# Attention and expert routing on one core: row transposes spread between layer products, second-layer weights moved up

## The chip, the cores and the metric

The kernel runs on one core of one Trainium2 chip. Five engines work side by side and are joined by semaphores only: TensorE (PE in the profile, PEld for its weight loads), VectorE (DVE), ScalarE (ACT), GpSimd (POOL) and SyncE (SP). The metric is device time in microseconds (us) from start to end of one execution; less is better.

## The reference, cut to what matters

```python
# q, k, v: (4, 8, 768, 64) float32; is_retrieval: 8 heads; n_sink = 4, window = 64
scores = scale * q @ k.T                       # scale = 1/sqrt(64)
keep = causal if is_retrieval[h] else causal & (is_sink | in_window)
a = softmax(where(keep, scores, -1e9))
x = (a @ v).transpose(0, 2, 1, 3).reshape(3072, 512)   # one row per token
for e in range(8):                              # domain_id: one expert per token
    rows = domain_id == e
    out[rows] = maximum(x[rows] @ w1[e], 0) @ w2[e]     # w1: 512x1024, w2: 1024x512
```

So there are two phases: masked attention, and a two-layer network in which each token goes to exactly one of eight experts.

## The kernel before, in words

**Attention.** It runs over 16 pairs of heads (four pairs for each of four batches). For pair n PE computes the scores into PSUM, ACT takes their exponential into the tiles eT, and PE multiplies pair n-1's tiles with v (`av_items`). DVE divides by the sums and writes fp16 rows xb. After each batch SP stores xb to the DRAM tensor x_tok (`store_x`). `hooks(n)` issues what belongs to pair n besides: SP's loads of q, k and v four pairs ahead, POOL's casts to fp16, and near the end POOL's first DMAs for the second phase. `routing_items` lets DVE work out, beside the attention, which token sits in which slot of which expert: map_i lists the rows to gather, out_i the rows to scatter to.

**Experts.** Each expert has 448 slots (CAP): 384 main ones in three groups of 128, and 64 spare ones. Experts are handled in pairs; a pair has seven groups of 128 slots, numbers 0 to 2 of its first expert, 3 to 5 of its second, and number 6 with the spare slots of both (the half group). For each group there are these steps:

- `load_xe(pr, g)`: POOL issues an indirect DMA that gathers 128 rows of x_tok into xe (L662). A gather given `nb=3` reads the first three batches only; slots that hold tokens of the last batch are gathered again after the last `store_x`.
- `x_transpose(pr, *gs)`: PE transposes the rows in 128x128 blocks, four for each group, into a PSUM tile xtp (L679); DVE copies them into xT (L692, and L686 for the half group).
- `layer1(e, c0, c1)`: PE computes 8 blocks of 128 hidden features, in four steps of two blocks (L707). Each step fills one tile of the pool `ps_s`, and ACT applies the ReLU into hT (L714).
- `layer2(e)`, `layer2_half(pr)`: PE computes 128x512 outputs into a tile of `ps_b` (L758, L772).
- `finish_group`: DVE copies the output to one of six oute buffers (L721), and POOL scatters its rows to `out` by an indirect DMA (L723).

`load_w(e, 1)` and `load_w(e, 2)` let POOL issue the load of an expert's first-layer or second-layer weight. The DMA casts it from float32 to fp16; the result has 1 MB. The pool `wpool` has four buffers for each of the two kinds.

PSUM is split in two pools: `ps_s` with three tiles of two banks (scores and first layer), and `ps_b` with two tiles of one bank (everything else, the transposes among it).

Each engine works its instructions off in the order in which the program text issues them (`manual_schedule`), so the text's order is the order on PE and in the POOL queue. POOL's DMAs share eight semaphores in turn; in the program as built, a POOL DMA therefore waits until the one eight places before it has landed. An oute buffer is written again only when the scatter six groups before has landed.

The order of the expert phase before: the transposes of pair 0's first four groups; `layer1` of experts 0 to 3 for the first 256 slots (EARLY; these tokens are all in the first three batches), with pair 1's transposes after expert 0; then for pairs 0 and 1 the late transposes (groups 2, 5, 6) and the other 192 slots. After that, for each pair: second layer, then all seven transposes of the pair two further on in a row, then that pair's first layer. Between these stand the weight loads, and behind the last three of them (after expert 3's second layer) `nc.gpsimd.drain()` (L889), in which POOL's sequencer stops.

At the very end a test of a flag (L907) would start a slow general path if an expert had more than 448 tokens; it is not taken here.

Of the kernel before, what the change touches and what calls it, by code (L numbers as in the profile page):

```python
# [21 lines left out]
def kernel(  # L22
# [164 lines left out]
    def load_w(e, which):  # L187
# [6 lines left out]
        else:  # L194
            t = wpool.tile([P, 2, 4, DM], FP16, tag="w2", name=f"w2_{e}")
# [475 lines left out]
    def x_transpose(pr, *gs):  # L671
# [3 lines left out]
        ps = ps_b.tile([P, 2, 4, P], FP16, tag="b", name=f"xtp_{pr}_{gs[0]}")  # L675
# [21 lines left out]
    def layer1(e, c0, c1):  # L697
# [3 lines left out]
        for f2 in range(4):  # L701
# [32 lines left out]
    def layer2(e):  # L734
        pr, i = divmod(e, 2)
        for g in range(3):
            if (e, g) == (E - 1, 2):
                o = opool.tile([P, DM], FP32, tag="oute", name="oute_last")
                ps = ps_s.tile([P, 1024], FP32, tag="sp", name="o2_last")
                for c in range(2):  # L740
                    for f in range(8):
                        nc.tensor.matmul(
                            out=ps[:, c * 512 : c * 512 + 256],
                            lhsT=hT_t[e][:, f, g * P : (g + 1) * P],
                            rhs=w_t[e, 2][:, f // 4, f % 4, c * 256 : (c + 1) * 256],
                            start=(f == 0),
                            stop=(f == 7),
                        )
                    for eng, x in ((nc.vector.tensor_copy, 0), (nc.scalar.copy, 128)):
                        eng(  # L750
                            out=o[:, c * 256 + x : c * 256 + x + 128],
                            in_=ps[:, c * 512 + x : c * 512 + x + 128],
                        )
                finish_group(pr, 3 * i + g, ps, o)
                continue
            ps = ps_b.tile([P, 512], FP32, tag="b", name=f"o2_{e}_{g}")
            for f in range(8):
                nc.tensor.matmul(  # L758
                    out=ps[:],
                    lhsT=hT_t[e][:, f, g * P : (g + 1) * P],  # L760
                    rhs=w_t[e, 2][:, f // 4, f % 4, :],
                    start=(f == 0),
                    stop=(f == 7),
                )
            finish_group(pr, 3 * i + g, ps)
# [39 lines left out]
    def hooks(n):  # L805
# [10 lines left out]
        ws = {6: (0, 1), 12: (1, 1)}  # L816
        if n in ws:
            load_w(*ws[n])
        if n == 12:
            for u in range(4):  # L820
                xe_of(u // 2, 3 * (u % 2))
                nc.vector.memset(xe_t[u][:, 0:2, :], 0.0)
        if n == 13:
            for g in (0, 1, 3, 4):
                load_xe(0, g, 3)
        if n == 14:
            load_w(2, 1)
            for g in (0, 1, 3, 4):
                load_xe(1, g, 3)
            load_w(3, 1)  # L830
# [8 lines left out]
    for n in range(NPAIR + 1):  # L839
# [5 lines left out]
        if n == NPAIR:  # L845
            steps = [A + B_]
        elif R == 3:
            steps = [A + T["q"], T["k"] + B_]
        else:
            h = len(B_) // 2  # L850
            steps = [A, T["q"] + B_[:h], T["k"] + B_[h:]]
# [7 lines left out]
    for g in ((0, 1), (3, 4)):  # L859
        x_transpose(0, *g)  # L860
    for g in (2, 5, 6):
        load_xe(0, g)
    load_w(0, 2)
    for g in (2, 5, 6):
        load_xe(1, g)
    load_w(1, 2)
    for g in range(4):
        load_xe(2, g)
    layer1(0, 0, EARLY)
    for g in ((0, 1), (3, 4)):  # L870
        x_transpose(1, *g)
    for e in range(1, N_EARLY):
        layer1(e, 0, EARLY)
    for pr in range(2):
        for g in (2, 5, 6):
            x_transpose(pr, g)
        for e in (2 * pr, 2 * pr + 1):
            layer1(e, EARLY, CAP)
# [124 lines left out]
```

## Time and profile before

| | us |
|---|---|
| median of 4 runs | 228.87 |
| lowest, highest | 227.42, 230.02 |
| the profiled execution | 228.89 |
| its span | 227.1 |
| PE busy | 192.4 (85%) |
| POOL busy | 115.8 (51%) |
| DVE busy | 100.3 (44%) |
| ACT busy | 91.8 (40%) |

The profile is one execution. Busy time is the sum of an engine's instructions; where an engine is the bound, its idle time makes the run longer, and elsewhere it costs nothing. "Span" runs from the first instruction to the last; the device time of the same execution is 1.8 us more. A line of a table by stretches gives the stretch and its length, then for PE, PEld, DVE, ACT and POOL the busy time and the number of instructions, then the clock that TensorE was granted (1.00 is full speed), the mean busy share of the 16 DMA engines, and GB/s. In a line in order of time, the bracket says how long the engine was idle before the instruction and which event ended that.

In the profiled execution the last attention product ends at about 98 us; the second layer of expert 0 starts at 133.17, that of expert 4 at 191.25; the last product ends at 221.0 and POOL's last scatter starts at 221.98.

### The profile page before, as it was taken

Reading aid. Unit: us, or ns where it says so; the run is one execution under the profiler, and the core shown is the slowest. Engines: PE = TensorE matmul, PEld = TensorE weight load, DVE = VectorE, ACT = ScalarE, POOL = GpSimd, SP = SyncE. Lnnn points to the kernel's source line nnn. Section 1 sums busy time; section 2 is a strip of 40 time slices with the busy share of each in tenths; the row PEclk is TensorE's granted clock in tenths of the full one; section 3 lists DMA queues with packets and bytes.
Section 4 is the critical chain, followed back from the end, with each engine's and each line's share of the span. In section 5 each row is a group of like instructions: output and inputs, shape, how many; then the busy total and the mean of one; then the engine's idle time right before and its main releaser. Section 6 shows DMA issues by size and latency. Waiting matters only on the chain. (4 is left out here: it accounts for less than half of the span.)

```text
span 227.1 us, 4809 instructions
## 1 busy us (share of the span) xinstructions
PE 192.4 (85%) x1959; PEld 123.2 (54%) x1959; DVE 100.3 (44%) x204; ACT 91.8 (40%) x120; POOL 115.8 (51%) x166
## 2 busy tenths in 40 slices
PE   1797869997799898769998899989999899999680
PEld 0455646665466566457998774546545365444240
DVE  2258998998857955550101213520135200443220
ACT  2674548765676785404564440035400155000000
POOL 2446865684555633870776606677176300067431
PEclk9999999999999999976999999999999699999978
DMA  6999999999999791399799997999999999324321
GB/s 204 324 310 300 295 305 270 321 282 269 292 334 332 129 271 38 79 198 294 172 193 195 258 245 225 172 250 250 169 193 274 287 214 216 63 115 161 130 89 51
DMA packets 42909, 49.79 MB, mean 219 GB/s; under 512 B 27263, under 2 KB 35712, under 8 KB 42882
## 3 DMA queue, kind: packets, MB, share of 16 engines
q0 software_dynamic: 7936, 26.75, 51.6%
q1 hardware_dynamic: 34802, 22.62, 35.1%
q8 instruction: 17, 0.28, 0.5%
q10 hardware_dynamic: 144, 0.07, 0.2%
q14 instruction: 10, 0.08, 0.1%
HBM read 56.76 MB, written 10.49 MB: 296 GB/s over the span
## 5 line engine op out<-in xcount | busy, mean ns | idle before, releaser
L342 ACT ACTIVATE eT<-sp 128x1024 f16<-128x1024 f32 (+2 forms) x68 | 57.4, 922 | 32.8 <-PE sp L305 31.9
L714 ACT ACTIVATE hT<-h 128x512 f16<-128x512 f32 (+2 forms) x48 | 31.8, 668 | 63.9 <-PE h L707 61.1
L707 PE MATMUL h<-xT,w 128*128 128x256 f16 (+2 forms) x384 | 54.0, 304 | 2.4 <-DVE xT L686 1.1
L723 POOL DMA_INDIRECT out_dram<-oute,out_i x27 | 27.0, 1000 | 47.6 <-DVE oute L721 44.6
L707 PEld LDWEIGHTS <-w 128*128 128x128 f16 x384 | 40.0, 116 | 15.4 <-issue 3.7
L758 PE MATMUL o<-w,hT 128*128 128x512 f16 x184 | 42.6, 389 | 2.3 <-DVE oute L721 2.3
L721 DVE COPY oute<-o 128x512 f32<-128x512 f32 x23 | 15.9, 691 | 58.5 <-PE o L758 57.5
L662 POOL DMA_INDIRECT xe<-x_tok,map_i x24 | 24.4, 1018 | 19.1 <-SPq L907 6.8
L758 PEld LDWEIGHTS <-hT 128*128 128x128 f16 x184 | 18.0, 100 | 25.3 <-issue 5.6
L305 PE MATMUL sp<-qT,kT 64*128 64x192 f16 (+8 forms) x276 | 23.9, 276 | 5.5 <-DVE kT L291 5.5
L395 PE MATMUL av<-ve,eT 128*128 128x65 f16 (+1 forms) x472 | 24.5, 195 | 3.2 <-DVE qT L291 1.9
L395 PEld LDWEIGHTS <-eT 128*128 128x128 f16 (+1 forms) x572 | 21.8, 100 | 8.6 <-issue 3.4
L158 POOL CAST q<-q 128x768 f16<-128x768 f32 x15 | 12.6, 837 | 22.6 <-DMA q<-in_q_dram 10.0
L305 PE MATMUL sp<-c16s 128*128 128x128 f16 (+1 forms) x132 | 22.6, 274 | 1.2 <-ACT eT L342 0.6
L178 POOL CAST ve<-v 128x384 f16<-128x384 f32 x32 | 16.4, 539 | 5.6 <-DMA v<-in_v_dram 5.5
L305 PEld LDWEIGHTS <-kT 64*128 64x128 f16 (+1 forms) x276 | 10.8, 96 | 15.6 <-DVE kT L291 9.1
L692 DVE COPY xT<-xtp 128x1024 f16<-128x1024 f16 (+1 forms) x16 | 8.4, 553 | 23.1 <-PE xtp L679 23.0
L408 DVE TENSOR_TENSOR xb<-av,rcp 128x384 f16<-128x384 f32 x32 | 17.8, 557 | 1.1
L291 DVE COPY kT<-tpk 128x768 f16<-128x768 f16 x16 | 15.2, 950 | 4.6 <-PE tpk L285 3.7
L291 DVE COPY qT<-tpq 128x768 f16<-128x768 f16 x15 | 14.3, 952 | 6.1 <-PE tpq L285 5.8
L158 POOL CAST k<-k 128x768 f16<-128x768 f32 x15 | 12.9, 857 | 5.8 <-PE tpk L285 4.4
L305 PEld LDWEIGHTS <-c16s 128*128 128x128 f16 x132 | 10.0, 102 | 6.0 <-issue 3.5
(83 smaller groups left out, 134.9 us busy)
## 6 DMA issues: line engine op xcount, KB each, us to landing
w<-in_moe_w_dram POOLq DMA_DIRECT2D x16, 1024.0 KB
q<-in_q_dram SPq DMA_DIRECT2D x16, 384.0 KB, 6.1
k<-in_k_dram SPq DMA_DIRECT2D x16, 384.0 KB, 5.9
v<-in_v_dram SPq DMA_DIRECT2D x32, 192.0 KB, 5.9
x_tok<-xb SPq DMA_DIRECT2D x4, 768.0 KB, 6.4
out_dram<-oute,out_i POOLq DMA_INDIRECT x27
xe<-x_tok,map_i POOLq DMA_INDIRECT x24
c16s<-c SPq DMA_DIRECT2D x1, 336.5 KB, 6.0
```

The lines of the kernel that those rows point to most:

```text
L158: eng.tensor_copy(out=t[:].rearrange("p t h d -> p h t d"), in_=q32_t[nm, n][:])
L178: nc.gpsimd.tensor_copy(out=ve_t[b][:, :, h, 0:D], in_=v_t[b, pi][:, hh])
L291: evac(out=d[:], in_=cell["ps"][:, 0:NSO].rearrange("d t p -> d p t"))
L305: nc.tensor.matmul(out=sp[rows, c : c + w], lhsT=lhsT, rhs=rhs, start=bank not in begun, stop=True, skip_group_check=True,)
L342: nc.scalar.activation(out=eT[n, r // 3][:, r % 3, c0:c1], in_=sp[:, c0:c1], func=AF.Exp, scale=scale)
L395: nc.tensor.matmul(out=ps[m0:m1, it, :], lhsT=eT[n, r // 3][:, r % 3, c : c + w], rhs=rhs, start=(x == 0), stop=(x == len(mms) - 1), skip_ ...
L408: nc.vector.tensor_tensor(out=xb[b][:, :, h * D : (h + 1) * D], in0=ps[:, :, 0:D], in1=rcp[:].unsqueeze(2).to_broadcast([P, NSO, D]), op=A ...
L662: nc.gpsimd.indirect_dma_start(out=xe_of(pr, g), out_offset=None, in_=x_d[0 : 1 + nb * S, :], in_offset=bass.IndirectOffsetOnAxis(ap=map_i ...
L707: nc.tensor.matmul(out=pv[:, a, c0:c1], lhsT=w_t[e, 1][:, c // 2, c % 2, fc * 512 + fr : (fc + 1) * 512 : 4], rhs=xT_t[e][:, c, c0:c1], st ...
L714: nc.scalar.activation(out=hT_t[e][:, 2 * f2 : 2 * f2 + 2, c0:c1], in_=pv[:, :, c0:c1], func=AF.Relu)
L723: inst = nc.gpsimd.indirect_dma_start(out=out, out_offset=bass.IndirectOffsetOnAxis(ap=out_i[:, s : s + 1], axis=0), in_=o[:], in_offset=None,
L758: nc.tensor.matmul(out=ps[:], lhsT=hT_t[e][:, f, g * P : (g + 1) * P], rhs=w_t[e, 2][:, f // 4, f % 4, :], start=(f == 0), stop=(f == 7),)
```

## The change

- `x_transpose` gets an option `wide`: its PSUM tile then comes from `ps_s` instead of `ps_b`.
- The transposes are no longer issued in blocks. Pair 0's first two groups come ahead of the last attention product (wide); the other early and late ones stand between half steps of `layer1`, which gets a parameter `f2s` for that; those of pairs 2 and 3 stand between the groups of `layer2` (wide), which is now called once for each group.
- Expert 2's first-layer weight is issued in `hooks(13)` (before: 14), and expert 0's second-layer weight in `hooks(14)`, behind the early gathers (before: after the last `store_x` and three more gathers). All early gathers are now issued in `hooks(14)`, and the clearing of their tiles goes from DVE (in `hooks(12)`) to POOL (in `hooks(14)`).
- The other second-layer weights each move up accordingly. Those of experts 6 and 7 take buffers of the first-layer kind (tag "w1"), which experts 4 and 5 leave free, and are issued after pair 1's half group and after expert 3's second layer.
- The gathers of groups 5 and 6 change places; expert 6's first-layer weight is issued between pair 3's gathers.
- The drain stands after the second group of expert 4's second layer, so behind two of its scatters.

```diff
-            t = wpool.tile([P, 2, 4, DM], FP16, tag="w2", name=f"w2_{e}")
+            tag = "w2" if e < 6 else "w1"
+            t = wpool.tile([P, 2, 4, DM], FP16, tag=tag, name=f"w2_{e}")
...
-    def x_transpose(pr, *gs):
+    def x_transpose(pr, *gs, wide=False):
...
-        ps = ps_b.tile([P, 2, 4, P], FP16, tag="b", name=f"xtp_{pr}_{gs[0]}")
+        if wide:
+            ps = ps_s.tile([P, 4, 4, P], FP16, tag="sp", name=f"xtp_{pr}_{gs[0]}")
+        else:
+            ps = ps_b.tile([P, 2, 4, P], FP16, tag="b", name=f"xtp_{pr}_{gs[0]}")
...
-    def layer1(e, c0, c1):
+    def layer1(e, c0, c1, f2s=range(4)):
...
-        for f2 in range(4):
+        for f2 in f2s:
...
-        ws = {6: (0, 1), 12: (1, 1)}
+        ws = {6: (0, 1), 12: (1, 1), 13: (2, 1)}
         if n in ws:
             load_w(*ws[n])
-        if n == 12:
+        if n == 14:
             for u in range(4):
                 xe_of(u // 2, 3 * (u % 2))
-                nc.vector.memset(xe_t[u][:, 0:2, :], 0.0)
-        if n == 13:
-            for g in (0, 1, 3, 4):
-                load_xe(0, g, 3)
-        if n == 14:
-            load_w(2, 1)
-            for g in (0, 1, 3, 4):
-                load_xe(1, g, 3)
-            load_w(3, 1)
+                nc.gpsimd.memset(xe_t[u][:, 0:2, :], 0.0)
+            for pr in range(2):
+                for g in (0, 1, 3, 4):
+                    load_xe(pr, g, 3)
+                load_w(*((3, 1), (0, 2))[pr])
...
-            steps = [A + B_]
+            steps = [[lambda: x_transpose(0, 0, 1, wide=True)] + A + B_]
...
-    for g in ((0, 1), (3, 4)):
-        x_transpose(0, *g)
-    for g in (2, 5, 6):
+    for g in (2, 6, 5):
         load_xe(0, g)
-    load_w(0, 2)
-    for g in (2, 5, 6):
+    load_w(1, 2)
+    for g in (2, 6, 5):
         load_xe(1, g)
-    load_w(1, 2)
+    load_w(2, 2)
     for g in range(4):
         load_xe(2, g)
-    layer1(0, 0, EARLY)
-    for g in ((0, 1), (3, 4)):
-        x_transpose(1, *g)
-    for e in range(1, N_EARLY):
-        layer1(e, 0, EARLY)
-    for pr in range(2):
-        for g in (2, 5, 6):
-            x_transpose(pr, g)
-        for e in (2 * pr, 2 * pr + 1):
-            layer1(e, EARLY, CAP)
-            if e < 2:
-                load_w(e + 4, 1)
-            if e == 0:
-                for g in range(4, NG):
-                    load_xe(2, g)
-    xes = lambda pr: [load_xe(pr, g) for g in range(NG)]
+    layer1(0, 0, EARLY, (0, 1))
+    x_transpose(0, 3, 4)
+    layer1(0, 0, EARLY, (2, 3))
+    layer1(1, 0, EARLY, (0, 1))
+    x_transpose(1, 0, 1)
+    layer1(1, 0, EARLY, (2, 3))
+    layer1(2, 0, EARLY, (0, 1))
+    x_transpose(1, 3, 4)
+    layer1(2, 0, EARLY, (2, 3))
+    layer1(3, 0, EARLY)
+    x_transpose(0, 2)
+    x_transpose(0, 6)
+    layer1(0, EARLY, CAP, (0, 1))
+    x_transpose(0, 5)
+    layer1(0, EARLY, CAP, (2, 3))
+    load_w(4, 1)
+    for g in range(4, NG):
+        load_xe(2, g)
+    layer1(1, EARLY, CAP, (0, 1))
+    x_transpose(1, 2)
+    x_transpose(1, 6)
+    layer1(1, EARLY, CAP, (2, 3))
+    load_w(5, 1)
+    layer1(2, EARLY, CAP, (0, 1))
+    x_transpose(1, 5)
+    layer1(2, EARLY, CAP, (2, 3))
+    layer1(3, EARLY, CAP)
     after = {
-        0: lambda: load_w(2, 2),
-        1: lambda: (load_w(3, 2), xes(3), load_w(6, 1), load_w(7, 1)),
-        2: lambda: load_w(4, 2),
-        3: lambda: (load_w(5, 2), load_w(6, 2), load_w(7, 2), nc.gpsimd.drain()),
+        0: lambda: load_w(3, 2),
+        1: lambda: (
+            [load_xe(3, g) for g in range(4)],
+            load_w(6, 1),
+            [load_xe(3, g) for g in range(4, NG)],
+            load_w(7, 1),
+        ),
+        2: lambda: (load_w(4, 2), load_w(5, 2)),
+        "h1": lambda: load_w(6, 2),
+        3: lambda: load_w(7, 2),
     }
     for pr in range(E // 2):
         a, b_ = 2 * pr, 2 * pr + 1
-        layer2(a)
+        xt = lambda *g: x_transpose(pr + 2, *g, wide=True) if pr + 2 < E // 2 else None
+        for g, gs in enumerate(((0, 1), (2,), (3, 4))):
+            layer2(a, g)
+            xt(*gs)
+            if (pr, g) == (2, 1):
+                nc.gpsimd.drain()
         if a in after:
             after[a]()
         layer2_half(pr)
-        layer2(b_)
+        if f"h{pr}" in after:
+            after[f"h{pr}"]()
+        xt(5)
+        layer2(b_, 0)
+        xt(6)
+        layer2(b_, 1)
+        layer2(b_, 2)
         if b_ in after:
             after[b_]()
         if pr + 2 < E // 2:
-            for g in ((0, 1), (2,), (3, 4), (5,), (6,)):
-                x_transpose(pr + 2, *g)
             layer1(a + 4, 0, CAP)
             layer1(b_ + 4, 0, CAP)
```

## The prediction

> **What bounds the kernel now.** I read the engine shares first, then the clock row, then the order of time on PE from the last attention product on, and last the POOL queue.
>
> ```profile
> PE 192.4 (85%) x1959; PEld 123.2 (54%) x1959; DVE 100.3 (44%) x204; ACT 91.8 (40%) x120; POOL 115.8 (51%) x166
> PEclk9999999999999999976999999999999699999978
> DMA  6999999999999791399799997999999999324321
> ```
>
> PE is the busiest engine, and where it stands still the run gets longer. The clock row has three dips; the DMA row is full up to slice 34 but for a hole at slices 15 to 18. So I cut the expert phase at PE's own borders (us; busy PE, PEld, DVE, ACT, POOL; then clock, DMA share, GB/s):
>
> ```profile
> 97.97:100.93 2.96, 1.42 (x18) 1.30 (x18) 1.55 (x4) 0.00 (x0) 2.35 (x4) 0.67 1.05 210
> 100.93:106.80 5.87, 5.87 (x34) 4.35 (x33) 0.69 (x1) 1.79 (x3) 0.52 (x1) 0.59 1.05 305
> 107.89:118.37 10.48, 10.48 (x100) 10.47 (x97) 0.89 (x2) 6.50 (x11) 8.31 (x9) 1.00 0.89 179
> 118.37:120.04 1.67, 0.99 (x14) 0.70 (x12) 1.10 (x4) 0.60 (x1) 1.37 (x2) 1.00 1.05 260
> 125.90:127.86 1.96, 0.99 (x15) 0.70 (x13) 1.20 (x4) 0.52 (x2) 1.01 (x1) 1.00 1.04 326
> 145.48:149.27 3.79, 2.21 (x29) 1.70 (x28) 3.08 (x7) 0.00 (x0) 2.75 (x4) 1.00 1.00 205
> 149.27:161.38 12.11, 12.11 (x65) 7.26 (x66) 0.05 (x1) 6.42 (x7) 7.99 (x9) 1.00 0.91 222
> 173.69:177.48 3.79, 2.21 (x30) 1.70 (x28) 3.08 (x7) 0.00 (x0) 3.04 (x5) 1.00 1.06 213
> 177.48:191.25 13.77, 13.77 (x64) 7.55 (x65) 0.05 (x1) 6.42 (x7) 0.59 (x1) 0.88 1.06 244
> 212.60:214.85 2.25, 0.00 (x0) 0.00 (x0) 0.74 (x2) 0.00 (x0) 0.00 (x0) 1.00 0.25 95
> 214.85:218.07 3.22, 3.22 (x8) 1.16 (x8) 0.54 (x1) 0.00 (x0) 1.97 (x2) 0.53 0.07 22
> ```
>
> Each stretch with transposes holds PE idle time (3.79 us, 2.21 busy), because two small PSUM banks make PE wait for DVE's copy. After such a stretch the same 64 products take 13.77 us at clock 0.88 instead of 12.11. At 212.60 PE waits 2.25 us for an output buffer, and 8 products then take 3.22 us. Last, POOL:
>
> ```profile
> 108.22 1.05 POOL L662 DMA_INDIRECT xe<-x_tok,map_i  x1 [6.78 <-SPq L907]
> 128.06 0.99 POOL L662 DMA_INDIRECT xeh<-x_tok,map_i  x1 [0.92 <-DMA w<-in_moe_w_dram]
> 199.83 1.07 POOL L723 DMA_INDIRECT out_dram<-oute,out_i  x1 [21.76 <-DVE oute L721]
> L889 POOLq DRAIN  x1: 22815/22815/22815, 176.1 to 176.1; - x1
> L998 POOLq DRAIN  x3: 50/109/3412, 222.9 to 226.8; - x3
> 194.50:201.00 6.50, 6.50 (x39) 2.81 (x38) 2.76 (x4) 0.00 (x0) 1.07 (x1) 1.00 0.06 11
> ```
>
> The late gathers wait for the last store of x (108.22). One gather waits for the weight eight DMAs before it, since POOL's DMAs share eight semaphores (128.06). The 21.76 us belong to the drain of L889, from 176.1 to 198.9; the DMA engines emptied at 194.5, with a remnant to 196. The end is POOL's last scatter at 221.98, 1.0 us behind PE's last product (221.0), and 5.1 us from there to the end of the span.
>
> **What the Trainium skill says.** "TensorE: Matmul & The Clock Gate", Part 1 (the HAM clock gate): after an idle window of about 3.4 us the array runs at half rate until it has been busy for one. Agrees: the clock is 0.50 from 99.0 to 105.8, 177.5 to 180.9 and 215.0 to 218.4. Part 4 of that page (PE-mode transpose): transposes don't count as busy in the same way. Agrees at 173.69; the equal stretch at 145.48 drew no dip, so the place in the window matters. "DMA: Bandwidth & Descriptors", Queues, rings and completion order: a DMA engine takes turns among queues, so a weight queued early slows SP's store of x. Same page, Anatomy of one DMA: a fixed part of some 2 us is mostly the write receipt. Agrees: the store's bytes stop at 85.5, the gather waiting for it starts at 88.18. No page bears on what a POOL drain waits for.
>
> **The change part by part.** Unit costs on PE at full clock: 109 ns per 256-wide product (10.48/96), 83 per 192-wide (5.31/64), 189 per 448-wide (12.11/64), 12.31 us for a pair's second layer, 68 ns per transpose (16 in 1.09).
>
> 1. *Spread transposes; wide ones in the three large PSUM banks.* The same 112 transposes stay on PE; their waits for DVE go under 0.7 to 1.7 us of products. DVE has room: a 0.69 us output copy and at most a 0.69 us transpose copy per 1.73 us group. Removed: 118.37: 1.67 - 12x0.068 = 0.85, and 0.55 of ragged start behind it; 125.90: 1.96 - 0.82 = 1.14; twice 3.79 - 28x0.068 = 1.9 each. Together 6.3.
> 2. *First transposes ahead of the last attention product.* 8 of them lie in PE's waits for ACT's exponentials (0.31 + 0.35 us), 8 come later (0.54): 2.96 - 0.54 = 2.4. Their gathers are issued about 1 us later than the 88.18 of before, at 89.2 and 90.6, and land by 95; PE asks at 95.6. If they are late, PE loses the difference; bounds 0 and 2, I take 0.
> 3. *Clock dips.* At 99.0 products now follow at once: 5.87 - 32x0.109 = 2.4. No transpose block at 174: 13.77 - 12.11 = 1.66. Bounds 0 and 4.1; I take 4.1, and charge one dip below.
> 4. *The stall near the end:* 2.25, and 3.22 - 1.73 = 1.49 of half clock behind it.
>
> Sum 6.3 + 2.4 + 4.1 + 3.7 = 16.5.
>
> 5. *DVE's clearing (2.1 us at 76 to 78) goes to POOL,* behind the last cast of v. It held back a PE wait of 0.60; bounds 0 and 0.6, taken 0. On POOL the trace shows only smaller clears; by width (four of 195 columns in 0.75 us) some 0.5 to 1.1 us each, 2 to 4.4 in all, beside the wait for the store of x.
> 6. *Weights earlier.* Expert 2's first and expert 0's second weight fill the DMA hole (share 0.23 from 86 to 97). A weight takes about 4.9 us of the DMA (1.05 MB at 215 GB/s), a gather about 0.6. After the store of x POOL issues as many DMAs as before, so the queue up to expert 5's first weight drains no earlier (about 138.5), while PE is ahead. New waits: expert 0's gathers lie behind the early weight (landing 113.5 to 114.2; PE asks at 113.6): 0.7. Expert 2's gather of rows 256 to 383 lies behind expert 1's second weight, landing at 120.4; PE asks at 118.85: 2.0 with its half group. At the first wide transposes 0.5. Sum 3.2.
> 7. *Last weights.* Their new waits, for the first layers of experts 4 and 5, are over by 155, long before POOL reaches them, so nothing queues behind them. No reason to be late: the first-layer weights of the last pair land near 160 and 166, asked for at 169; the last second-layer weight is issued at 171 and moved by 187, asked for at 199.
>
> PE starts the second layer at 128.2 (133.17 before), the last two pairs at 181.1 (191.25), and ends at 206.9: 14.1 earlier; the difference from 16.5 - 3.2 is rounding along the way.
>
> 8. *The drain, now behind two scatters.* Behind it on POOL stand twelve scatters; DVE's copies need their six buffers, and PE needs DVE. The two are issued near 183.6 and 185.3 and move behind the last weight, to 188.3. With 3 to 4 us on top, as before (194.5 or 196 to 198.9), the drain ends at 192. Twelve scatters follow at 1.30 us: 192.9 + 11x1.3 = 207.2 for the last. PE permits 207.9. Both bounds meet here, so the drain is no longer free: each us that it ends after 193 is a us at the end.
>
> Span 207.9 + 5.1 = 213.0. Outside the span lie 228.89 - 227.1 = 1.8: 214.8. One clock dip, likely at the waits near 118 to 121, adds 1.7: **216.5**, 5.4% below the profiled execution, which equals the median of 228.87. A difference under about 1% could not be told from no change.
>
> **Rivals.**
> - *Gathers starve PE.* The store of x shares the DMA engines with two weights. If it lands 3 us later, the gathers behind it do too, PE waits 3 us more, and the clock dips there by 2.4: 216.5 + 5.4 = 222. For it: the DMA share is about 1.05 from 97 to 108. Against: two weights lay beside that store before as well.
> - *The drain takes its time whatever the DMAs do.* If its 22.8 us are work for the DMAs issued so far and not a wait for the last to land, it runs from 185.3 to 208.1. The first scatter starts at 209.0; its buffer is free by 212.9 (before, a copy waiting for the one issued at 199.83 ran at 203.76). PE has stopped, restarts at 213.6 at half clock: 3.7 for the half group, 1.73 twice, 2.93 for the last, 1.0 to the scatter at 224.7, and 5.1 + 1.8: 231.6, slower than before. It decides once the drain ends after 206. For it: 22.8 us is long beside the 3.4 of the drain at the end. Against: it ended 3 us behind the DMA's last bytes, and the final one (222.9 to 226.3) lasts just as long as one scatter needs to land.
> - *The dips stay.* The clock's window may catch the short attention products at 96 to 98 anyway: 216.5 + 2.4 = 219.
>
> **How the numbers follow.** The forecast with the dips staying (212 to 220): 0.62. Starved gathers (220 to 226): 0.15. Long drain: 0.14. Better than 212, if the dip I charged stays away and DVE's 0.6 counts: 0.04. Near no change, by several waits: 0.05. The range 212 to 227 leaves out the long drain and the best case. Faster by over 1% (below 226.6): 0.79; slower: 0.14; within 1%: 0.07.
>
> **What would show it.** In the profile after: transposes of 8 or 4 between products without DVE waits; no clock dip before 110 nor at 170 to 185; the second layer begins near 128 and its last two pairs near 181; a PE wait of about 2 us near 119; the drain ends some 3 us behind the last weight's bytes, near 192, and scatters follow at 1.3 us without a hole. Wrong if the drain lasts over 20 us, if PE waits for xe for more than 5 us in all, or if PE's last product lies after 214.

## The result, and the profile after

Where it was first measured, the changed kernel takes 226.14 us (median of 12 runs, 224.59 to 231.35), the kernel before in the same sessions 229.37 (17 runs): ratio 0.9875, 95% interval 0.9833 to 0.9917. A gain of 1.25%, where 5.4% was forecast. The profiled execution took 226.17 us with a span of 224.3. Some executions of each kernel come out over 1.5% slower than its fastest one; medians here are of all runs, ratios and their intervals of the others alone.

The gain differs from chip to chip, so that comes first. The unaltered changed kernel was run again in three of the sets of runs below, each on a chip of its own and beside the kernel before:

| where | before, us | changed, us | ratio, 95% interval |
|---|---|---|---|
| first measurement | 229.37 | 226.14 | 0.9875 (0.9833 to 0.9917) |
| set 3 | 225.36 | 215.68 | 0.9557 (0.9497 to 0.9618) |
| set 4 | 224.91 | 216.93 | 0.9629 (0.9588 to 0.9671) |
| set 5 | 231.37 | 225.93 | 0.9773 (0.9704 to 0.9841) |

Where the kernel before is quick (225 us), the change brings about the time that was predicted (216.5); where it is slow (229 and 231 us), about half of the gain or more is lost. These are called quick and slow chips below. No chip served two sets, so what belongs to the chip and what to the hour can't be told apart. What follows reads the first measurement, and then what sets it apart.

First the page of the changed kernel (share of engines, clock, DMA):

```profile
PE 189.4 (84%) x1959; PEld 124.2 (55%) x1959; DVE 97.8 (44%) x200; ACT 91.9 (41%) x120; POOL 119.6 (53%) x170
PEclk9999999999999999979996999999999999999955
DMA  6999999999999899599549999996999999504321
```

PE is 3.0 us less busy (192.4 before): the clock's dip at slice 32 has gone and that of slices 18 and 19 is shorter, but there is a new one at slice 22, and the last two slices are slower. The DMA row has a hole at slices 20 and 21, later than the one before. Cut at PE's borders again (us; busy PE, PEld, DVE, ACT, POOL; clock, DMA share, GB/s):

```profile
97.44:132.95 35.51, 31.35 (x305) 29.51 (x304) 6.26 (x15) 16.91 (x31) 17.36 (x19) 0.90 0.85 192
132.95:146.83 13.88, 13.88 (x95) 7.10 (x94) 6.40 (x12) 0.52 (x2) 7.29 (x9) 1.00 1.03 242
172.81:184.92 12.11, 12.11 (x66) 7.25 (x65) 0.69 (x1) 6.42 (x7) 2.81 (x3) 1.00 1.06 217
209.11:216.46 7.35, 1.04 (x10) 0.79 (x9) 1.25 (x3) 0.27 (x1) 3.95 (x4) 0.83 0.36 136
```

The middle does what was forecast: second layer and transposes of a pair take 13.88 us without idle time (12.31 + 3.79 = 16.10 before), and the 64 products behind it 12.11 at full clock (13.77 before). The first line and the last hold the waits. In order of time:

```profile
116.59 0.40 PE L683 MATMUL xtp<-c16s,xeh 128*128 128x128 f16 x4 [1.69 <-DMA xeh<-x_tok,map_i]
124.03 0.40 PE L683 MATMUL xtp<-c16s,xe 128*128 128x128 f16 x4 [0.62 <-DMA xe<-x_tok,map_i]
125.89 0.40 PE L683 MATMUL xtp<-c16s,xeh 128*128 128x128 f16 x4 [1.47 <-DMA xeh<-x_tok,map_i]
216.46 1.86 PE L745 MATMUL o_last<-w,hT 128*128 128x256 f16 x8 [6.31 <-ACT oute_last L753]
```

and POOL, with its drain:

```profile
111.57 1.05 POOL L663 DMA_INDIRECT xe<-x_tok,map_i  x1 [11.92 <-SPq L930]
200.19 0.98 POOL L727 DMA_INDIRECT out_dram<-oute,out_i  x1 [9.65 <-DVE oute L725]
219.29 0.98 POOL L727 DMA_INDIRECT out_dram<-oute_last,out_i  x1 [5.20 <-DVEq L930]
L912 POOLq DRAIN  x1: 10026/10026/10026, 189.3 to 189.3; - x1
```

The store of x holds the late gathers to 111.57 (108.22 before). The second layer starts at 132.95, where it started before (133.17): 7.06 us behind the start of the transposes that waited last for a gather (125.89). The drain ends at 199.3 (198.9 before). After it come eleven scatters, 1.29 us apart, PE's last half group waits 6.31 us, and the last scatter starts at 219.29, 2.7 us earlier than before.

The same on the quick chip of set 3, from a profiled execution of 214.26 us:

```profile
95.62:127.96 32.34, 27.97 (x307) 27.12 (x305) 5.67 (x14) 16.87 (x31) 19.68 (x21) 1.00 1.00 225
103.96 0.38 PE L683 MATMUL xtp<-c16s,xe 128*128 128x128 f16 x4 [2.46 <-DMA xe<-x_tok,map_i]
120.91 0.40 PE L683 MATMUL xtp<-c16s,xeh 128*128 128x128 f16 x4 [0.88 <-DMA xeh<-x_tok,map_i]
106.28 1.05 POOL L663 DMA_INDIRECT xe<-x_tok,map_i  x1 [6.50 <-SPq L930]
208.35 0.98 POOL L727 DMA_INDIRECT out_dram<-oute_last,out_i  x1 [0.30 <-issue]
L912 POOLq DRAIN  x1: 8987/8987/8987, 184.3 to 184.3; - x1
```

| | forecast | first measurement | set 3 |
|---|---|---|---|
| second layer of expert 0 | 128.2 | 132.95 | 127.96 |
| second layer of expert 4 | 181.1 | 184.92 | 179.93 |
| drain ends | 192 | 199.3 | 193.3 |
| last scatter | 207.9 | 219.29 | 208.35 |
| span | 213.0 | 224.3 | 212.5 |

Luck has a part in how close set 3 comes. PE waits 3.0 us there for early gathers (2.46 and 0.53), which step 2 put at nothing, and 0.9 for late ones, where step 6 had 3.2 us of waits; and the clock dip that was charged with 1.7 us doesn't come.

### The profile page after: what moved, and what is told of

It reads as the page before. It is cut to its first block, busy times and chain, and to the rows that moved or that the text cites. A ratio compares the mean times of both kernels' runs of the same rounds, so it can differ in the third digit from the quotient of the medians.

```text
span 224.3 us, 4806 instructions
## 1 busy us (share of the span) xinstructions
PE 189.4 (84%) x1959; PEld 124.2 (55%) x1959; DVE 97.8 (44%) x200; ACT 91.9 (41%) x120; POOL 119.6 (53%) x170
## 5 line engine op out<-in xcount | busy, mean ns | idle before, releaser
L711 PE MATMUL h<-xT,w 128*128 128x256 f16 (+2 forms) x384 | 53.2, 301 | 0.9 <-DVE xT L696 0.5
L711 PEld LDWEIGHTS <-w 128*128 128x128 f16 x384 | 40.7, 117 | 11.6 <-issue 1.0
L761 PE MATMUL o<-w,hT 128*128 128x512 f16 x184 | 41.9, 379 | 0.0
L761 PEld LDWEIGHTS <-hT 128*128 128x128 f16 x184 | 17.5, 98 | 19.8 <-issue 0.8
L306 PE MATMUL sp<-qT,kT 64*128 64x192 f16 (+8 forms) x276 | 24.5, 280 | 4.0 <-DVE kT L292 4.0
L306 PE MATMUL sp<-c16s 128*128 128x128 f16 (+1 forms) x132 | 23.1, 277 | 1.3 <-ACT eT L343 0.8
L306 PEld LDWEIGHTS <-kT 64*128 64x128 f16 (+1 forms) x276 | 11.0, 97 | 14.2 <-DVE kT L292 7.0
L753 ACT COPY oute_last<-o_last 128x128 f32<-128x128 f32 x2 | 0.5, 266 | 32.5 <-DVE oute_last L753 32.5
```

Of the source, the lines that this page charges most:

```text
L306: nc.tensor.matmul(out=sp[rows, c : c + w], lhsT=lhsT, rhs=rhs, start=bank not in begun, stop=True, skip_group_check=True,)
L711: nc.tensor.matmul(out=pv[:, a, c0:c1], lhsT=w_t[e, 1][:, c // 2, c % 2, fc * 512 + fr : (fc + 1) * 512 : 4], rhs=xT_t[e][:, c, c0:c1], st ...
L761: nc.tensor.matmul(out=ps[:], lhsT=hT_t[e][:, f, g * P : (g + 1) * P], rhs=w_t[e, 2][:, f // 4, f % 4, :], start=(f == 0), stop=(f == 7),)
```

## The experiments

A set is a group of kernels run on one chip, beside runs of the kernel before. Across sets only the ratios are compared.

### Set 1: what gives the time back?

The kernel before took 227.54 us here. The first idea was that two things undo the gain: expert 0's second weight in front of the store of x, and the drain with its burst of scatters.

**The changed kernel without its drain.**

```diff
-            if (pr, g) == (2, 1):
-                nc.gpsimd.drain()
```

> The changed kernel without the drain that stands behind the second scatter of expert 4. Theory A (the drain holds POOL until all its DMAs have landed, and the twelve scatters behind it then come in one burst whose landings are late): POOL scatters at PE's pace of 1.73 us, PE no longer waits for output buffers (1.2 and 6.3 us before), its last product ends near 211, the last scatter starts near 212, and the time is about 219 us. Rival B (the stream of weights sets the end whatever the drain does): the scatters only queue behind the weights until 195, and the time stays at 225 to 227. Rival C (a drain's time grows with the DMAs since the last one): the drain at the end of the program takes 10 to 20 us instead of 3.4, and the time is 228 or more.

222.9 us, ratio 0.9761 (0.9637 to 0.9886). The scatters follow PE from 188.81 on, no closer than 1.7 us, and PE's long wait is gone; no output copy of expert 4 or later starts more than 0.2 us behind its PE group. The last scatter starts at 212.53. But from there to the end of the span it is 7.8 us instead of 5.0, so the time is not the 219 us of theory A: the final drain takes 6.08 us, not 3.22.

**Expert 0's second-layer weight back behind pair 0's late gathers,** the other second-layer weights each one place back; the drain stays.

```diff
-                load_w(*((3, 1), (0, 2))[pr])
+                if pr == 0:
+                    load_w(3, 1)
...
     for g in (2, 6, 5):
         load_xe(0, g)
-    load_w(1, 2)
+    load_w(0, 2)
...
-        0: lambda: load_w(3, 2),
-        1: lambda: (
+        0: lambda: load_w(2, 2),
+        1: lambda: (
+            load_w(3, 2),
```

> The changed kernel with expert 0's second-layer weight back behind pair 0's late gathers, and the three that follow it back in the places of the kernel before; drain and transposes as in the change. Theory A (that weight, queued ahead, holds up the last store of x): the store lands within 8 us of its issue (10.3 with the change), POOL resumes near 108 instead of 111.6, PE waits less than 1 us for gathers (3.8 with the change), and the second layer starts near 129 instead of 133. The time falls by 1 to 4 us, since the drain and the scatters still follow the stream of weights. Rival B (the store is late for another reason): POOL resumes at 111 again and the second layer starts at 133.

223.56 us, ratio 0.9797 (0.971 to 0.9883). POOL resumes at 107.42 and the second layer starts at 129.06, as theory A had it, though PE still waits 2.8 us for late gathers. Then pair 3's gathers, now one more weight behind, cost a PE wait of 2.35 us at 163.63 and a half-rate window; the second layer of expert 4 starts at 185.18.

**Eight output buffers instead of six.**

```diff
-tc.tile_pool(name="moe_out", bufs=6)
+tc.tile_pool(name="moe_out", bufs=8)
```

> The changed kernel with eight output buffers instead of six; the drain stays. Theory A (PE's 6.3 us at the end are a wait for a buffer whose scatter lands 9 us late): PE ends near 211, the last scatter follows the others at 1.3 us and starts near 214.4 instead of 219.3, and the time is about 221 us. Rival B (the late landings themselves set the end): the last scatter starts earlier, but lands 7 to 9 us after its issue, and the time stays above 224.

225.26 us, ratio 0.9881 (0.979 to 0.9971), as the changed kernel where it was measured; the unaltered changed kernel was not run in this set, so this one stands in for it. All runs of the later weight, and those of no drain that count in the ratio, are below its lowest (224.14). PE still waits 6.24 us before its last half group. The last three output copies start 1.2, 2.4 and 5.6 us behind the PE group they copy, and 1.3, 2.4 and 5.7 in the changed kernel with six buffers: buffers that come free earlier change nothing.

**The kernel before without its drain.**

```diff
-        3: lambda: (load_w(5, 2), load_w(6, 2), load_w(7, 2), nc.gpsimd.drain()),
+        3: lambda: (load_w(5, 2), load_w(6, 2), load_w(7, 2)),
```

> The kernel before without its drain. Theory A (the drain as a burst maker): POOL scatters pair 2's first group near 194 instead of 199.8, PE's wait of 2.25 us near 212 and the half clock behind it go, and the time falls by 3 to 4 us, to about 225.5. Rival B (weights set the end): within 1 us of the kernel before. Rival C (the drain's work only moves to the end): slower than before by 5 us or more.

226.7 us, ratio 0.9958 (0.9919 to 0.9997). PE's wait at 212.6 goes, as theory A said, and the last scatter starts at 218.22 (221.98 before); but again the final drain takes 6.08 us (3.41), and the time is within 1 us of the kernel before, as in B. What a drain on the way costs, it saves for the most part at the end. The profile (of an execution of 227.86 us) shows one thing more. Up to the late gathers this is the kernel before, and POOL is held as long as in the changed one:

```profile
111.54 1.05 POOL L662 DMA_INDIRECT xe<-x_tok,map_i  x1 [11.10 <-SPq L907]
```

### Set 2: both edits together, and more slots

The kernel before took 224.9 us here. The first kernel joins the two single edits of set 1; the third adds to it `nc.gpsimd.drain()` right behind the last `store_x`; the fourth moves pair 3's gathers in it:

```diff
         1: lambda: (
+            [load_xe(3, g) for g in range(5)],
             load_w(3, 2),
-            [load_xe(3, g) for g in range(4)],
+            [load_xe(3, g) for g in range(5, NG)],
             load_w(6, 1),
-            [load_xe(3, g) for g in range(4, NG)],
```

The second is the changed kernel with slots for fourteen outputs, so that no copy behind the drain has to wait for a scatter behind the drain:

```diff
+    BIG = [(2, 5)] + [(3, g) for g in (0, 1, 2, 6, 3, 4, 5)]
...
+            big_t[k // 4] = wpool.tile([P, 4, DM], FP32, tag="w1", name=f"big_{k // 4}")
+        return big_t[k // 4][:, k % 4, :]
...
+        if o is None and (pr, g) in BIG:
+            o = big_out(BIG.index((pr, g)))
+            nc.vector.tensor_copy(out=o[:], in_=ps[:])
```

> After with both single edits together: expert 0's second-layer weight back behind pair 0's late gathers, and no drain between the scatters. Theory (two separate givebacks, one at the store of x, one at the drain; they add): second layer of expert 0 starts at 129, as in the run with the weight alone; scatters follow PE from about 185 on without a hole; but pair 3's gathers stand behind one more weight and PE waits for one of them (2.35 us and a half-rate window of 1.6 in the run with the weight alone), so the gain shows only in part: last scatter near 211, span near 219, 221 us. If the gather wait is absent: 217. Rival (what bounds the end is the DMA stream of weights, not the order): no better than the run without the drain alone, 222.9.

217.16 us, ratio 0.9599 (0.9505 to 0.9693): better than expected. The profile is of its slowest execution (221.29 us): PE waits 5.28 us for an early gather, which no run of set 1 had, and the second layer starts at 131.52.

> After, drain left where it is; the last eight outputs go to two freed weight buffers (eight 2 KB slots), so that no output copy of the last fourteen has to wait for a scatter of the burst behind the drain. Theory (the late copies at the end, 1.3, 2.4 and 5.7 us behind PE, wait for output buffers, whose scatters land late in a burst; eight buffers were still too few): copies follow PE within 0.2 us, PE's last product ends near 211, and POOL's twelve scatters at 1.30 us from 200.2 set the end: last scatter near 214.5, 219.6 span, about 221.5 us. Rival (DVE is held off by POOL's back-to-back descriptor writing, whatever buffers there are, since eight buffers gave the same three delays): the three delays stay, last scatter near 219, 226 us.

217.5 us, ratio 0.9669 (0.9593 to 0.9744). No late copy, last scatter at 210.53, 14.2 us behind the first after the drain. It looked like a proof of the slots. But this kernel's POOL also resumed at 106.73 with the weight still in front of the store, and up to there it is the changed kernel. So the chip was suspected.

> The first kernel of this set plus a drain ahead of pair 0's late gathers, where POOL waits for the store of x anyway. Without any drain on the way the final one lasted 6.08 us in two kernels; with one on the way 3.2 to 3.4. Theory A (the final drain pays for DMAs issued since the drain before, so an early one takes part of it, whatever stands behind): final drain 3.3 to 5 us, 1 to 2.8 us faster than the first kernel. Theory B (what counts is how many DMAs lie between, some 50 here against 12 or 14): 6.1 us again, same time as the first kernel. The early drain itself ends with the landing of two first-layer weights near 107 to 110: 0 to 3 us on the late gathers.

217.9 us, ratio 0.9654 (0.9578 to 0.9729). The final drain took 5.35 us, between the two theories, and the time is that of the first kernel: an early drain takes only a little off the last one.

> The first kernel of this set, with five of pair 3's gathers ahead of expert 3's second-layer weight and the other two ahead of expert 6's first-layer weight. Theory: PE's wait of 2.35 us for pair 3's rows and the half-rate window behind it (stage of 18.0 us instead of 13.9) go: second layer of expert 4 at 181, last scatter at 208, span 216, 217.5 us. Rival (the weights behind are then late): the same 4 us come back as a wait for expert 3's second weight near 163 or for expert 6's first weight near 169; about 221.

220.94 us, ratio 0.9789 (0.9713 to 0.9866), slower than the first kernel. The wait for pair 3's rows went, as the theory said. The profile, again of the slowest execution (224.53 us), has no wait for either of the two weights that the rival named, but PE waits 0.89 and 1.72 us for output buffers in the second layers of experts 5 and 6. Whether that is the whole loss isn't shown.

### Set 3: the parts alone, with the changed kernel beside them

The kernel before took 225.36 us here.

> The changed kernel unaltered, beside the three that follow, since chips differ by a per cent or two (before: 224.9 us in the last set, 229.4 where the changed kernel was measured). Theory: ratio to before 0.9875 as measured, with POOL held by the last store of x for 11 to 12 us and a stall of the last output copies. Rival (what differed in the last set, a store that held POOL for 6.5 to 8.5 us and a wait of PE for early gathers of 3 to 5 us, belongs to the chip and not to the edits): this run shows the same two marks, second layer of expert 0 at 130 to 131.

215.68 us, ratio 0.9557. Neither the marks of the first measurement nor its ratio. The rival, that the marks go with the chip, holds: POOL was held for 6.50 us and PE waited 3.0 us for early gathers, though the second layer starts at 127.96 and not at 130 to 131.

**Transposes only:** PE's order of the changed kernel; loads, tags, clears and drain as before.

```diff
         ws = {6: (0, 1), 12: (1, 1)}
...
         0: lambda: load_w(2, 2),
         1: lambda: (load_w(3, 2), [load_xe(3, g) for g in range(NG)], load_w(6, 1), load_w(7, 1)),
         2: lambda: load_w(4, 2),
         3: lambda: (load_w(5, 2), load_w(6, 2), load_w(7, 2), nc.gpsimd.drain()),
```

> The PE part of the change alone: transposes spread and wide, groups 6 and 5 exchanged; all loads, clears and the drain where they were before. Theory (the spread transposes carry the whole gain, and the earlier weights give some of it back): as good as after or better, ratio 0.98; second layer of expert 0 near 129 to 131; then PE waits some 4 us for a gather of pair 3; stall and burst behind the drain as in after, last scatter 216 to 218. Rival (without the earlier weights PE would run into the weight stream): slower than after, ratio 0.99 to 1.0, with waits for second-layer weights at 129 or 137.

223.29 us, ratio 0.9911 (0.9865 to 0.9958): the theory was wrong, and the rival right in size but not in cause. PE never waits for a weight. It reaches the second layer of expert 4 at 181.89 (191.25 in the profile of before), and then runs into the drain:

```profile
L900 POOLq DRAIN  x1: 22804/22804/22804, 174.2 to 174.2; - x1
201.56 5.75 PE L760 MATMUL o<-w,hT 128*128 128x512 f16 x16 [5.46 <-DVE oute L724]
```

The drain ends at 197.0, as early as the weights allow; six outputs fill the buffers behind it, and PE waits 5.46 us and runs at half rate afterwards.

**Loads only:** POOL's order of the changed kernel, drain behind two scatters, transposes in blocks as before.

> The POOL part alone: loads, clears and drain as in after, transposes in blocks as before. Theory: the weight stream ends when it ended before (194 to 196), PE's time is as before, so ratio 1.00, between 0.99 and 1.01; the drain now stands behind two scatters, or ahead of all of them where PE is late, and ends near 199, no change. Rival (the earlier weights are worth something by themselves: drain over by 192): ratio 0.985 or less.

222.76 us, ratio 0.9866 (0.9812 to 0.992), close to the rival's value, though not for its reason. The drain is issued at 195.5, behind scatters that PE's order delivers late, and takes 6.22 us, to 201.7; PE does not wait for output buffers at the end, but it is late: second layer of expert 4 at 191.09.

So the parts bring 0.9% and 1.3% alone and 4.4% together. Each alone is held by the other's bound: with the transposes alone PE is early and the drain is not; with the loads alone the drain no longer holds PE up, but PE is late.

**Transposes only, and no drain.**

> The PE part alone as above, and no drain. Theory: scatters follow PE, no stall at the end; last scatter 211 to 212, final drain 6.08 us, ratio 0.96 to 0.965, the same as with expert 0's weight moved back in the changed kernel and no drain (0.960). Rival (the earlier weights are needed once the drain is out of the way): ratio 0.975 or more, with PE waits for weights.

219.37 us, ratio 0.9714 (0.9649 to 0.9779), between the two forecasts: 3.9 us better than with the drain, and 3.7 behind the changed kernel. PE waits for no weight here either. It waits 4.1 us for early gathers, and the second layer of expert 4 starts at 182.82 (179.93 in the changed kernel); its final drain takes 6.08 us (3.89).

### Set 4: single edits on a quick chip

The kernel before took 224.91 us here. All four run side by side: the changed kernel, fourteen slots, no drain, later weight.

> The changed kernel unaltered, as the base of this set. Theory (two kinds of chips): either the marks of the first measurement (POOL held by the store of x for 11 to 12 us, output copies at the end 1.3, 2.4 and 5.7 us late, 3 to 5 of 16 increments recorded for a scatter's landing; ratio to before 0.985 to 0.99), or those of the set before this one (6.5 us, no late copy, 16 of 16; ratio 0.955 to 0.96). Rival (the time is spread evenly between the two): a ratio near 0.97 with one mark of each kind.

216.93 us, ratio 0.9629; a quick chip again (POOL held 7.28 us, second layer of expert 4 at 181.61).

> The changed kernel with fourteen output slots, beside the changed kernel on one chip. Theory (slots count only where landings are late): on a chip of the quick kind within 1% of the changed kernel, since its copies wait 0.2 us at most there; on a chip of the slow kind 4 to 5 us faster than it, the three late copies gone, last scatter at the drain's end plus 11 x 1.29 us. Rival (late copies have another cause than slots): no gain on a slow chip either.

217.3 us, ratio 0.9656 (0.9606 to 0.9706): no difference, as expected on a quick chip. PE's wait of 1.30 us before the half group goes; POOL's burst sets the end either way.

> The changed kernel without its drain, beside it on one chip. Theory: scatters follow PE, last one 1 us behind PE's last product, then the final drain of 6.08 us. On a quick chip PE ends near 205.5 in both, so span 206.9 + 7.8 = 214.7 against 212.5: 2 us slower than the changed kernel. On a slow chip 3 to 4 us faster, as in the first set. Rival (the drain costs wherever the kernel runs): faster than the changed kernel on a quick chip too.

219.03 us, ratio 0.9725 (0.9676 to 0.9774): 2.1 us slower than the changed kernel, 2 forecast. The final drains of this kernel and of the changed one:

```profile
L1019 POOLq DRAIN  x3: 50/109/6076, 210.1 to 216.8; - x3
L1021 POOLq DRAIN  x3: 50/109/3935, 210.5 to 215.1; - x3
```

The longest of the three in each line is the one that counts. Removing the drain makes the last scatter start 1.9 us earlier (209.27 against 211.15) and the last drain 2.1 us longer. The profiled execution of this kernel was 1 us later at expert 4, ahead of the edit, so part of its lateness isn't the drain's.

> The changed kernel with expert 0's second-layer weight back behind pair 0's late gathers, drain kept, beside it on one chip. Theory: on a quick chip the store of x lands in time with the weight ahead of it too, and the weight behind the gathers makes every later load one weight later, so pair 3's gather is waited for: 2 to 4 us slower than the changed kernel. On a slow chip 2 to 2.5 us faster, as in the first set. Rival (the early weight holds up the store on any chip): faster than the changed kernel on a quick chip too.

217.85 us, ratio 0.9696 (0.9655 to 0.9737): 0.9 us slower than the changed kernel where 2 to 4 were forecast, and as the intervals overlap, not shown to be slower. POOL resumes at 107.11 (107.44 with the weight ahead): at the store the edit gains next to nothing here. The wait that was named is there:

```profile
163.30 0.40 PE L683 MATMUL xtp<-c16s,xe 128*128 128x128 f16 x4 [1.87 <-DMA xe<-x_tok,map_i]
```

### Set 5: a slow chip, slots beside the changed kernel

The kernel before took 231.37 us here.

> The changed kernel once more, as the base for the run beside it. Three chips out of three of the sets that held it, or its early part, since the second set were quick (ratio 0.956 and 0.963 where it ran itself). Theory: which of two kinds of chip runs it decides; either 0.955 to 0.965 or 0.985 to 0.99, with the marks named for its third run. Rival: anything between.

225.93 us, ratio 0.9773. The ratio lies between the two kinds, as the rival allowed, but all marks of the first measurement are back: POOL held for 12.86 us, copies late at the end, PE's last half group 5.06 us late.

> Fourteen output slots beside the changed kernel. Theory: on a quick chip no difference within 1% (0.9656 against 0.9629 in the set before); on a slow chip 4 to 5 us faster than the changed kernel, since the three late copies go, and last scatter 14.2 us behind the drain's end. Rival: no gain on a slow chip either, so that late copies have another cause than slots.

225.25 us, ratio 0.9712 (0.9615 to 0.9809), within its interval the same. Here the rival won: the copies of this kernel wait for nothing but PE, and are late all the same. Its 13th output, by PE and by DVE (start, length, engine):

```profile
206.26 3.63 PE L772 MATMUL o<-w,hT 128*128 128x512 f16 x16
209.72 1.04 PE L756 MATMUL o_last<-w,hT 128*128 128x256 f16 x8
214.28 0.69 DVE L733 COPY big<-o 128x512 f32<-128x512 f32 x1 [4.28 <-remote]
```

PE leaves this output at 209.72 and goes on to the next; DVE copies it at 214.28. PE's semaphore update for it stands in the trace at 214.26. In the trace of the same kernel on the quick chip of set 4 this group ends at 203.98, its update stands at 204.15, and DVE follows at once. So it is not a slot that comes late, but PE's signal. On the quick chip the same two instructions read:

```profile
203.98 1.04 PE L756 MATMUL o_last<-w,hT 128*128 128x256 f16 x8
204.18 0.69 DVE L733 COPY big<-o 128x512 f32<-128x512 f32 x1 [1.04 <-PE o L772]
```

## Why the prediction was wrong at the first measurement

**In short.** What the prediction said of PE's own work held. The step that failed is the date in step 7, the last weight moved by 187: it rested on a last store of x that lands as early as before (step 6). The store landed later, the stream of weights lost its lead, the last weight was moved at 194 to 195, and the drain of step 8 ended at 199.3 instead of 192. Besides, the sum had no term for PE's signals to DVE, which put the last scatter another 4.9 us late.

**What held.** Step 1 (spread transposes) and the dip of step 3 behind the last block: the stages of 13.88 and 12.11 us above. Step 2: the first layer starts at 97.44 (100.93 before; but at 102.81 on the slow chip of set 5, where PE waits 2.03 us for DVE among the last attention products). Step 5 cost nothing that can be seen. Step 7: no product waits for one of the last two weights. Of the prediction's readings two were loose, and little rests on them: the store's last packet ends at 86.8 and not at 85.5, and it has landed by 87.28, 0.45 us later, so that line doesn't show a fixed part of 2 us; and PE was forecast 14.1 us earlier where the terms sum to 13.3, more than rounding makes.

**Step 3, the dip at 99.** Forecast to go, with "the dips stay" as a rival of 2.4 us. It stayed (clock 0.5 from 97.9 to 101.2), and the one charged at 118 to 121 came too. The idle window of about 3.4 us that the prediction named doesn't fit either of them: of the 3.41 us ahead of the first PE is busy for 2.46, of those ahead of the second for 1.34. Against the quick chip PE is busy 31.35 instead of 27.97 us in the stretch to the second layer. But these 3.4 us are not what makes the second layer late: at 125.89, behind both dips, PE waits 1.47 us for a gather, and a faster PE would have waited longer.

**Step 6, the store of x.** The working took the waits behind the late gathers from a store that lands when it landed before. Sized at 3.2 us, PE's gather waits measured 3.8: this term was nearly right. What was not: POOL resumes at 111.57 and not at or before 108.22, 3.35 us late, and for 8 us the DMA engines are two thirds idle (share 0.34 from 108 to 112 and 0.29 to 116, against 0.83 and 0.99 on the quick chip). The second layer of expert 0 is late by 4.75 us against the forecast. It follows POOL: from POOL's resuming to the end of PE's last wait for a late gather it is 14.32 us here and 14.63 on the quick chip (106.28 to 120.91), and from there to the second layer 7.06 and 7.05. This is what the rival of starved gathers had said of the store, 3 us later, though PE's waits did not grow by 3 us.

Three parts of the delay against the quick chip (5.3 us) can be looked at. First, the store is issued at 100.5, on the quick chip at 96.7, since DVE got the last attention products late:

```profile
98.88 0.20 DVE L408 RECIPROCAL rcp<-av 128x6 f32<-128x6 f32 x1 [1.50 <-remote]
99.72 0.20 DVE L408 RECIPROCAL rcp<-av 128x6 f32<-128x6 f32 x1
```

PE's last of these products ended before 97.44, where it starts the first layer; its two signals stand in the trace at 98.86 and 99.69, and POOL is issuing gathers at 1.3 us meanwhile. That is the same lateness as at the end. Second, the store's bytes waited. The DMA queues of the changed kernel in the 3 us from 101 to 104 and in the 4 us from 104 to 108 (packets, MB, share of the 16 engines; q0 is POOL's, q1 SP's):

```profile
q0 software_dynamic: 180, 0.60, 103.8%
...
q0 software_dynamic: 122, 0.50, 66.7%
q1 hardware_dynamic: 86, 0.53, 33.6%
```

In the first stretch SP's queue moves nothing at all; its first packet starts at 104.7. The prediction leaned on the Trainium skill, "DMA: Bandwidth & Descriptors", Queues, rings and completion order, for engines taking turns; here SP's queue got no turn for 4.2 us. On the quick chip it got none for 4.3 us after the issue at 96.7, so this wait belongs to the kernel and only its start to the chip. Third, from the first packet to the last it takes 5.8 us, on the quick chip 4.1.

How much of this is the change's doing stays open. In set 1, on one slow chip, the later weight cut the wait for the first packet to 1.1 us. But the kernel before, in the profile shown there, was held to 111.54 as well: the 108.22 that the prediction built on was one execution's value.

**Step 8, the drain.** "It ends with the last weight's bytes plus 3 to 4 us" was right: the bytes end near 195, the drain at 199.3. "The last weight is moved by 187" (step 7's date) was not: the stream had lost its lead in the hole at 110. By 105 us POOL's queue had moved 5.80 MB (4.15 before), by 120 us 7.19 MB (6.94 before, 8.29 on the quick chip), and from there to 185 the DMA engines are full (share 1.02 to 1.06) but for 147 to 159 (0.83), so it was not made good. That makes the first scatter after the drain 7.3 us late (200.19 instead of 192.9). The rival of a drain that takes its time whatever the DMAs do falls: it took 10.0 us, not 22.8.

**Step 4, the stall near the end,** was to go; it came back larger, 1.23 us at 203.80 and 6.31 at 216.46, then half clock. With PE's signals on time the last scatter would lie at 200.19 + 11 x 1.29 = 214.4; it lies at 219.29, 4.9 us later.

The sum: 7.3 by the drain and 4.9 by the late signals, less the 0.7 by which the forecast let PE and not POOL set the last scatter, is 11.5; the span missed the forecast by 11.3. The time missed it by less, 9.7, because the 1.7 charged for a dip was not needed on top. The working said that each us of the drain after 193 is a us at the end, and that held. It had no term for signals.

**What stays open.** Why PE's signals come late on some chips. They do so while POOL issues indirect DMAs back to back: in set 1, on one slow chip, they are 1.2 to 5.6 us late behind the drain's burst of scatters (eight buffers), and within 0.2 us where the drain is left out and the scatters follow PE. In the stretches with late signals these traces hold only 3 to 5 of the 16 increments of most landings, where the quick chips' hold all 16. So the recording may take part: every timed execution lists a clock and a span, and was then recorded too; whether this matters wasn't tried. Nor does the trace, whose ends of PE's products are modelled, tell a late signal from a product that really ended late. None of the kernels here is shown to beat the changed one on both kinds of chip: no drain and the later weight helped in set 1 (0.976 and 0.980, against 0.988 with eight buffers); in set 4 no drain cost 2.1 us and the later weight gained nothing; their union (0.960 in set 2) was not run beside the changed kernel.

## What to carry to other kernels

- Two bounds that meet at the end, here PE's output and a drain behind the weight stream, have to be moved together. Alone the halves brought 0.9% and 1.3%, together 4.4%: before giving up on a part, ask what held it.
- When the time differs from a well-founded forecast, run the unaltered kernel on another chip before explaining, and look whether the kernel before shows the same mark. Set 1 explained by edits what went with the chip, and set 2 seemed to prove it. Both edits that helped on the slow chip brought nothing on the quick one.
- Read who is late. A copy that waits points at its buffer, but eight or fourteen of them changed nothing; the next product on PE already running while its predecessor's copy waits pointed to a late signal.

## What the runs showed of the hardware

- While POOL issued scatters every 1.29 us, PE's last signals to DVE came 1.2 to 5.7 us late on the slow chips and within 0.2 us on the quick ones, at equal bytes and packets. On a slow chip, with scatters no closer than 1.7 us, they came within 0.2 us.
- A store of 768 KB issued by SP moved no packet for 4.2 us (slow chip) and 4.3 us (quick chip) while POOL's queue of weights and gathers kept the DMA engines busy.
- The kernel's final drain lasts 6.08 us in the six kernels without a drain on the way, 5.35 with one before the late gathers, and 3.2 to 4.2 with one ahead of the last twelve to fourteen scatters (5.33 once). A drain in the middle of POOL's queue lasts as long as what is in flight: 10.0 us, 9.0 and 22.8, each ending 2.7 to 3.0 us behind the last packet of POOL's queue.
